# First queries on the ACT queue, half of each Q copy on GpSimd, and the ReLU tiles moved by 128 bytes

## The chip, the cores and the metric

The kernel runs on one core of one Trainium2 chip. The metric is the device time of one execution in microseconds (us); lower is better. The core has five engines that matter here: PE (TensorE, the matrix unit), DVE (VectorE), ACT (ScalarE), POOL (GpSimd) and SP (SyncE, which in this kernel only issues DMAs). Each runs its own instructions in order and waits on semaphores of the others.

## The reference

Two blocks follow each other, all in float32. The first is a gated linear recurrence over 4 batches, 8 heads, 768 positions and a head size of 48:

```python
for t in range(S):
    state = alpha[:, :, t, :, None] * state + np.einsum('bhd,bhe->bhde', k[:, :, t], v[:, :, t])
    y[:, :, t] = np.einsum('bhd,bhde->bhe', q[:, :, t], state)
```

Its output, with the heads laid side by side, is `x`, 3072 rows of 384. The second block is a mixture of four experts, whose shares are normalised probabilities:

```python
p = domain_probs / (domain_probs.sum(-1, keepdims=True) + 1e-09)
for e in range(E):
    h = np.maximum(x @ w1[e], 0.0)
    out += p[:, e:e + 1] * (h @ w2[e])
```

Here `w1[e]` is 384 by 1024 and `w2[e]` is 1024 by 384.

## The kernel before, in words

**Units and groups.** The recurrence is cut into 24 units, one for each chunk of 128 positions and each batch. Units are gathered into groups for the expert block: the first group has two units (256 rows of `x`), the next five have four (512 rows) and the last has two. A group can go through the experts when its units are done, and while the PE works on the experts of one group, the units of the next are worked off between its matmuls.

**One unit (`attention`, L273).** The generator loads alpha, K, Q and V of its chunk, and turns alpha, K and Q on the PE (L270) so that channels lie on partitions: `AT` (L281), `KT` (L286) and `QT` (L300, alpha times Q). Then it goes through seven levels, which double the distance over which the decays are multiplied up. At each level `copy_q` (L314) copies the half of `QT` that is needed into a block `qb`, in two copies of 64 partitions each (L321): heads are kept in pairs, and each member of a pair has its own half of the partitions and of the block. `next_q` (L324) multiplies the same half of `QT` in place (L328), so it has to wait until both copies have read the old values, and builds the next decays (L330). `next_k` (L333) copies one half of `KT` into a new tile (L340) and multiplies the other half into it (L341). The scores of a level come from the PE (`products`, L348) and are taken into `near` under a mask (`take`, L358, which reads `masks`); the last level writes `far` (L403) and the pieces are joined in `lat` (L416, L421). `result` multiplies them with V (L443) and ACT copies the outcome into the group's `x` (L459). `turn_keys` and L478 make the state for the next chunk.

For the first unit `alone` is true (L296): nothing else runs yet. Its KT copies at L340 already go to POOL (L339); its Q copies all go to ACT.

**Experts.** `up` computes `x @ w1` in tiles `one` and `two`, and `down` computes `h @ w2` (L650). From the second group on the numbers are split into parts that the PE's faster float32r form holds exactly enough: `one` and `two` at L557, then ACT copies `one` to `t` (L568), DVE adds `two` (L570), ACT writes the ReLU of `t` to `hT` (L595), and DVE makes two more parts of it in `hT` (L597, L603). `hT` is the tile of the ReLU values: four buffers from the pool `hid`. In `down` a block of 128 rows of `hT` is the stationary operand of the PE and 384 columns of `w2` are the moving one. The first group runs in plain float32 (L549, L551, and L650 on `hT` with no split).

**Weights.** In the first group, SP loads the pieces of `w1` straight from the input (L214, L215), four pieces of three DMAs of 128 KB; raw `w2` pieces land in unused parts of `hT` (L217). ACT and DVE split them, POOL writes the split form to a kept buffer in DRAM (L233), and later groups load it from there (L196).

**The start, in order.** ACT issues the DMAs of `ident` and `masks`. POOL clears tiles. SP issues alpha, K, Q (L167) and V (L172 to L174) of unit 0, then the same of unit 1, then the probabilities (L749), then the twelve DMAs of the first four `w1` pieces. Unit 1's alpha, K and Q land in one `hT` buffer. PE fills the time with matmuls on zeros (`idle`, L760), which are counted out by hand: 7 ahead of the turn of alpha, 2 ahead of that of K, 3 ahead of that of Q, 21 ahead of unit 1's first turn. Each of these is two records in the trace. After the first unit, `up` of the first group starts on the first 128 rows (L549).

**Memory.** Tiles lie in a partition in the order of the pools: `const`, `wts`, `work`, `hid`. The last tile of `work` is `x_raw`, and `hid` begins right behind it with the four buffers of `hT`, followed by `acc`.

Order is set by the program text (a manual schedule): on each engine, instructions stand as the generators are called.

Of the kernel before, what the change touches and what calls it, by code (L numbers as in the profile page):

```python
# [10 lines left out]
F32 = mybir.dt.float32  # L11
# [9 lines left out]
def kernel(  # L21
# [37 lines left out]
    nc = tc.nc  # L59

    B, H, S, D = q.shape
    E, DM, F = moe_w1.shape
    P = 128
# [5 lines left out]
    KC = DM // P  # L69
    FCH = F // P  # L70
    NT = B * P
# [6 lines left out]
    assert DM % P == 0 and F % (P * NQ) == 0 and DM <= 512 and KC * QF == FPQ * DM  # L78
    FINE = 1 + 1 / 4096
    TRIM = 1 - 1 / 8192  # L80

    j = np.arange(P)[:, None] % HALF
    n = np.arange(QUAD)[None, :]
    mask_np = np.stack([(j // (2 * m) == n // m) & (j % (2 * m) < m) for m in LEVELS[:6]],
                       1).astype(np.uint8)
# [5 lines left out]
    work = ctx.enter_context(tc.tile_pool(name="work", bufs=2))  # L91
# [5 lines left out]
    masks = const.tile([P, 6, QUAD], U8, name="masks")  # L97
# [33 lines left out]
    def raw(u, nm):  # L131
        return values[u % 2] if nm == "v" else apart[nm] if u == 1 else early[nm]

    xTs = {}
    xraws = {}
# [24 lines left out]
    def load(u, names):  # L160
        if u >= len(units):
            return
        cb, b = units[u]
        for nm in names:
            src = srcs[nm][b, :, cb * P:(cb + 1) * P, :].rearrange("h s d -> s h d")
            if nm != "v":
                nc.sync.dma_start(out=raw(u, nm)[:, :, :D], in_=src)  # L167
                continue

            pairs = raw(u, nm).rearrange("p (a i) d -> p a i d", i=2)  # L170
            src = src.rearrange("p (a i) d -> p a i d", i=2)
            nc.sync.dma_start(out=pairs[:, :, 0, :D], in_=src[:, :, 0])  # L172
            nc.sync.dma_start(out=pairs[:, :, 1, :TAIL], in_=src[:, :, 1, QUAD:])
            nc.sync.dma_start(out=pairs[:, :, 1, TAIL:D], in_=src[:, :, 1, :QUAD])  # L174
# [46 lines left out]
    def split_piece(l, i):  # L221
# [3 lines left out]

        nc.scalar.activation(out=top, in_=whole, func=ACT.Copy, scale=TRIM)
        yield
        nc.scalar.activation(out=dif, in_=whole, func=ACT.Copy, scale=TRIM * 4096)
        yield
# [43 lines left out]
    def attention(u):  # L273
        cb, b = units[u]
# [21 lines left out]
        alone = u == 0  # L296
# [17 lines left out]
        def copy_q(li):  # L314
            m = LEVELS[li]
            qv = halves(QT, m)[:, :, :, 1, :]
            qb = free.popleft()
            qbs.append(qb)
            for i in range(2):
                rows = slice(HD * i, HD * (i + 1))  # L320
                nc.scalar.copy(out=qb[rows, :, i, :].rearrange("p a (b r) -> p a b r", r=m),  # L321
                               in_=qv[rows])

        def next_q(li):  # L324
            m = LEVELS[li]
# [88 lines left out]
        for s in range(2):  # L414
            rows = slice(HALF * s, HALF * (s + 1))
            nc.scalar.copy(out=parts[:HALF, :, s, :, HALF:], in_=far[rows])  # L416
        yield
        for s in range(2):
            rows = slice(HALF * s, HALF * (s + 1))
            copy = nc.vector.tensor_copy if alone and s else nc.scalar.copy  # L420
# [8 lines left out]
        def result():  # L429
            yps = ps.tile([P, KC, P], F32, name="yps", tag="w")  # L430
            for c in range(KC):


                if c < 2:
                    now = [[(2 * c + j // 2, j % 2, (0, HD + TAIL)[j % 2], 2 * QUAD * (j % 2))
                            for j in range(4)]]
                    turns = ([(True, now[0])] if cb > 0 else []) + [(False, now[0])]
                else:
                    turns = [(True, [(p, 0, 0, QUAD) for p in range(NP)])] if cb > 0 else []
                    turns += [(False, [(p, i, QUAD + TAIL * i, 0) for p in range(NP)]) for i in range(2)]  # L440
                for n, (past, turn) in enumerate(turns):
                    for j, (p, i, in_v, in_st) in enumerate(turn):
                        nc.tensor.matmul(  # L443
                            yps[QUAD * j:QUAD * (j + 1), c, :],
                            lhsT=flat_st[:, p, in_st:in_st + QUAD] if past
                            else flat_v[:, p, in_v:in_v + QUAD],
                            rhs=QT[:, p, :] if past else lat[:, 2 * p + i, :],
                            start=(n == 0), stop=(n == len(turns) - 1))
            gi, slot = place[cb, b]
            if slot == 0:  # L450
                if gi == 0:
                    xTs[gi] = work.tile([P, 3, KC, NT], F32R, name="xT", bufs=1)
                    xraws[gi] = xTs[gi][:, 2].bitcast(F32)
                elif gi < LAST:
                    xraws[gi] = work.tile([P, KC, NT], F32, name="x_raw", bufs=1)
                else:
                    xraws[gi] = []
            if gi < LAST:
                nc.scalar.copy(out=xraws[gi][:, :, slot * P:(slot + 1) * P], in_=yps)  # L459
            else:  # L460

                xraws[gi].append(AT)
                nc.scalar.copy(out=AT[:, :KC, :], in_=yps)
# [10 lines left out]
        if cb < NCB - 1:  # L474
# [5 lines left out]
            for i in range(2):  # L480
                rows = slice(HD * i, HD * (i + 1))
# [17 lines left out]
    def split_x(gi, step):  # L499
# [7 lines left out]
        for kc in range(KC) if step == 0 else [step - 1]:  # L507
# [3 lines left out]
            for x, out in pieces:  # L511
                if step == 0:
                    nc.scalar.activation(out=out[0], in_=x, func=ACT.Copy, scale=TRIM)
                else:
# [78 lines left out]
    def hidden_parts(x, parts):  # L593
        top, low, dif = parts
        nc.scalar.activation(out=top, in_=x, func=ACT.Relu, scale=TRIM)  # L595
        yield
# [136 lines left out]

    with tc.manual_schedule():
        nc.scalar.dma_start(out=ident_all, in_=nc.inline_tensor(ident_np, name="ident_c").ap())
        nc.scalar.dma_start(out=masks, in_=nc.inline_tensor(mask_np, name="masks_c").ap())
        nc.gpsimd.memset(sts[B - 1], 0.0)
        for nm in "akq":
            for r in (early[nm], apart[nm]):
                nc.gpsimd.memset(r[:, :, D:], 0.0)  # L740
        nc.gpsimd.memset(lat[HALF:, :, :HALF], 0.0)
        for t in values + blocks:
            nc.gpsimd.memset(t, 0.0)
        for t in sts[:-1]:
            nc.gpsimd.memset(t, 0.0)

        load(0, "akqv")
        load(1, "akqv")
        nc.sync.dma_start(out=p_all, in_=moe_domain_probs.rearrange("(n p) e -> p n e", p=P))  # L749
        for i in range(NQ):  # L750
            load_piece(0, i)

        idle = ps.tile([P, P], F32, name="idle", tag="g", bufs=4)
        zeros = sts[B - 1].rearrange("p a i d -> p (a i d)")[:, :P]

        def fill(n):
            for _ in range(n):
                nc.tensor.matmul(idle, lhsT=zeros, rhs=zeros, start=True, stop=True)  # L760

        runs = [attention(u) for u in range(len(groups[0]))]
        fill(7)
        for u, n in ((0, 2), (0, 3), (0, 4), (0, 5), (0, 5), (0, 4), (0, 3), (1, 0), (0, 0), (0, 2),
                     (0, 2), (1, 2), (0, 2), (1, 0), (0, 0), (0, 4), (0, 4), (0, 0)):
            next(runs[u])
            fill(n)
        norm_probs()

        span = cost(0, 0, 0) * FCH / 2 + cost(1, 0, 0)  # L770
        waiting.extend((span * (k + 1) / 15, u, runs[u])
                       for k, u in enumerate([1, 1, 1, 0, 1, 0, *[1] * 8]))
        for fc in range(FCH):
            up(0, 0, fc, slice(0, 1))
            advance(cost(0, 0, 0) / 2)
        down(0, 0, [0], deque())
        while waiting:
            next(waiting.popleft()[2], None)
        clock = 0.0
        waiting.extend((1.0 + k, 1, runs[1]) for k in range(2))  # L780
        waiting.extend(deal())

        for (gi, e), after in zip(tasks, [*tasks[1:], (None, None)]):
            rest = gi == e == 0
            for fc in range(FCH):
                up(gi, e, fc, slice(1, len(groups[0])) if rest else None)
                advance(cost(0, gi, e) / (2 if rest else 1))
            each = len(groups[gi]) if split2(gi, e) else 1
            turns = [range(k, k + each) for k in range(rest, len(groups[gi]), each)]
            for k, slots in enumerate(turns):  # L790

                between = deque()
                if after[1] == 0:

                    for step, at in enumerate((0.0, 0.3, 0.42, 0.54) if gi == 0 else
                                              (0.0, 0.6, 0.7, 0.78)):
                        at = at * len(turns) - k
                        if 0 <= at < 1:
                            between.append((at, lambda step=step: split_x(after[0], step)))
                down(gi, e, slots, between)  # L800
        while stores:
            stores.popleft()()
# [28 lines left out]
```

## Time and profile before

| What | Value |
|---|---|
| Median of 4 runs | 1057.53 us |
| The runs | 1057.48, 1057.49, 1057.57, 1059.46 us |
| The profiled execution | 1059.58 us, of which the instructions span 1057.8 us |
| PE busy | 1039.5 us, 98% of the span |
| DVE, ACT, POOL busy | 782.0, 565.1, 35.5 us |
| Granted TensorE clock | 1.00 |
| DMA | 251.66 MB, mean 238 GB/s |
| `down` in float32r (L650) | 1872 matmuls, 347.4 us |
| `up` in float32r (L557) | 960 + 480 matmuls of the four-unit groups, 253.1 + 136.4 us |

In the profile a group of instructions is named by its line, its engine, its operation and out<-in tiles. `PEld` is the load of the stationary operand, which goes beside matmuls; `SPq` and `ACTq` are issues of DMAs by those engines. The mean duration of a matmul in the profile contains its way through the array, so the time that a row of matmuls takes is read from their starts, not from the mean. A releaser after `<-` names what ended an engine's idle time.

### The profile page before, as it was taken

To read this page: it belongs to the slowest core of one execution; us is meant where nothing else is said; L and a number is where in the kernel's file an instruction comes from. 1 tells how busy PE (TensorE), PEld (TensorE's weight loads), DVE (VectorE), ACT (ScalarE), POOL (GpSimd) and SP (SyncE) were. 2 spreads that over 40 slices of the span, in tenths; PEclk is the share of its full clock that TensorE was granted. 3 is DMA by queue.
4 is the path that set the end of the run, shared out by engine and by line. 5 is a ranking of instruction groups with operands and counts; after the bars stand their busy time and mean duration, and the time that the engine had idled before them with its cause. 6 is when DMAs were issued, how large, how long until landed. Compare 5 with 4: busy or idle time off the path is not lost.

```text
span 1057.8 us, 21578 instructions
## 1 busy us (share of the span) xinstructions
PE 1039.5 (98%) x8498; PEld 904.9 (86%) x8498; DVE 782.0 (74%) x1620; ACT 565.1 (53%) x1195; POOL 35.5 (3%) x77
## 2 busy tenths in 40 slices
PE   8899999999999999999999999999999999999998
PEld 8777777687877899898898898998989989898988
DVE  5578777668879778778877777986877875656565
ACT  4687776585665654445546536555474453323232
POOL 3000010000001000000000000000000000000000
PEclk9999999999999999999999999999999999999999
DMA  7596799997878956857759659576594454454531
GB/s 116 168 335 209 237 309 361 318 338 240 274 269 292 372 198 223 318 163 287 289 178 335 236 161 358 182 275 251 168 364 188 173 209 179 179 186 173 206 152 46
DMA packets 158837, 251.66 MB, mean 238 GB/s; under 512 B 120112, under 2 KB 135344, under 8 KB 136208
## 3 DMA queue, kind: packets, MB, share of 16 engines
q1 hardware_dynamic: 152688, 208.87, 57.9%
q0 software_dynamic: 5760, 41.29, 9.8%
q8 instruction: 67, 1.10, 0.4%
q14 instruction: 34, 0.28, 0.1%
q10 hardware_dynamic: 288, 0.12, 0.1%
HBM read 207.79 MB, written 42.47 MB: 237 GB/s over the span
## 4 chain that ended last, share of the span: by engine, by line
PE 82%; DMA 5%; DVE 4%; ACT 4%; SPq 3%; issue 1%; POOL 0%; ACTq 0%; DVEq 0%; POOLq 0%
PE ops L650 34%; PE one L557 23%; PE two L557 11%; PE sc L348 5%; PE yps L443 3%; PE tp L270 3%; SPq L214 2%; ACT qb L321 2%; DMA w<-in_moe_w_dram 2%; PE sps L478 1%; PE far L403 1%; PE one L549 1%; DMA w<-kept 1%; DMA kept<-w 1%; DMA rq<-in_q_dram 1%
## 5 line engine op out<-in xcount | busy, mean ns | idle before, releaser
L650 PE MATMUL ops<-w,hT 128*128 128x384 f32 x1872 | 347.4, 340 | 0.2 <-DVE hT L603 0.2
L650 PEld LDWEIGHTS ops<-w,hT 128*128 128x128 f32 x1872 | 325.4, 188 | 4.7 <-ACT t L568 0.6
L557 PE MATMUL one<-xT,w 128*128 128x512 f32 x960 | 253.1, 399 | 1.2 <-DVE xT L252 0.5
L557 PEld LDWEIGHTS one<-xT,w 128*128 128x128 f32 x960 | 175.8, 188 | 40.0 <-ACT t L568 1.5
L568 ACT ACTIVATE t<-one 128x512 f32<-128x512 f32 (+1 forms) x192 | 106.9, 557 | 176.2 <-PE one L557 170.8
L321 ACT COPY qb<-QT 64x256 f32<-64x256 f32 x336 | 136.5, 406 | 74.2 <-DVE QT L300 40.8
L597 DVE SCALAR_TENSOR_TENSOR hT<-t,hT 128x512 fp32r<-128x512 f32 (+1 forms) x172 | 110.5, 643 | 68.3 <-ACT hT L595 66.4
L570 DVE TENSOR_TENSOR t<-t,two 128x512 f32<-128x512 f32 (+1 forms) x172 | 109.4, 636 | 58.0 <-ACT t L568 29.1
L595 ACT ACTIVATE hT<-t 128x512 fp32r<-128x512 f32 (+1 forms) x172 | 101.8, 592 | 85.9 <-DVE t L570 84.9
L557 PE MATMUL two<-xT,w 128*128 128x512 f32 x480 | 136.4, 393 | 0.0
L557 PEld LDWEIGHTS two<-xT,w 128*128 128x128 f32 x480 | 90.1, 188 | 20.2 <-DVE acc L679 0.3
L603 DVE SCALAR_TENSOR_TENSOR hT<-hT 128x512 fp32r<-128x512 f32 (+1 forms) x172 | 101.0, 635 | 0.0
L650 PE MATMUL ops<-hT 128*128 128x384 f32 x288 | 100.6, 491 | 0.1
L358 DVE COPY_PREDICATED near<-masks,sc 128x256 f32<-128x256 uint8 x144 | 77.0, 535 | 19.2 <-PE sc L348 16.3
L328 DVE TENSOR_TENSOR QT<-QT,dec 128x256 f32<-128x256 f32 x144 | 61.1, 425 | 35.5 <-ACT qb L321 34.7
L348 PEld LDWEIGHTS sc<-qb,KT 128*64 128x64 f32 x2304 | 72.7, 138 | 9.3 <-issue 4.7
L348 PE MATMUL sc<-qb,KT 128*64 128x64 f32 x2304 | 77.2, 223 | 2.6 <-ACT qb L321 2.6
L650 PEld LDWEIGHTS ops<-hT 128*128 128x128 f32 x288 | 52.1, 190 | 29.1 <-issue 0.4
L679 DVE SCALAR_TENSOR_TENSOR acc<-ops,p_all,acc 128x384 f32<-128x384 f32 x82 | 49.9, 615 | 29.7 <-PE ops L650 28.5
L341 DVE TENSOR_TENSOR KT<-KT,dec 128x256 f32<-128x256 f32 x144 | 60.2, 418 | 0.0
L340 ACT COPY KT<-KT 128x256 f32<-128x256 f32 x138 | 57.4, 416 | 3.1
L549 PE MATMUL one<-xT,w 128*128 128x256 f32 (+1 forms) x240 | 46.8, 341 | 1.7 <-DMA w<-in_moe_w_dram 1.1
(90 smaller groups left out, 935.2 us busy)
## 6 DMA issues: line engine op xcount, KB each, us to landing
w<-kept SPq DMA_DIRECT2D x144, 1152.0 KB
kept<-w POOLq DMA_DIRECT2D x32, 1152.0 KB, 7.4
hT<-in_moe_w_dram SPq DMA_DIRECT2D x32, 384.0 KB
w<-in_moe_w_dram SPq DMA_DIRECT2D x48, 128.0 KB
ra<-in_alpha_dram SPq DMA_DIRECT2D x23, 192.0 KB
rk<-in_k_dram SPq DMA_DIRECT2D x23, 192.0 KB
rq<-in_q_dram SPq DMA_DIRECT2D x23, 192.0 KB
out_dram<-acc POOLq DMA_DIRECT2D x18, 192.0 KB, 6.7
```

The lines of the kernel that those rows point to most:

```text
L321: nc.scalar.copy(out=qb[rows, :, i, :].rearrange("p a (b r) -> p a b r", r=m), in_=qv[rows])
L328: nc.vector.tensor_mul(qv, qv, spread(dv[:, :, :, 0], m))
L341: nc.vector.tensor_mul(new[:, :, :, 0, :], old[:, :, :, 0, :], spread(halved(decs[li])[:, :, :, 1], m))
L348: nc.tensor.matmul(out[HALF * s:HALF * (s + 1), 2 * p:2 * p + 2, :], lhsT=KTs[li][:, p, HALF * s:HALF * (s + 1)], rhs=qbs[li][:, p, :, QUA ...
L358: nc.vector.copy_predicated(near.rearrange("p a (b two r) -> p a b two r", two=2, r=m)[:, :, :, 1, :], mk.unsqueeze(1).broadcast_to([P, H, ...
L557: nc.tensor.matmul(out, lhsT=w[:, part, kc], rhs=x_part(gi, part, kc), start=(part == terms[0] and kc == 0), stop=(part == terms[-1] and k ...
L568: nc.scalar.activation(out=t, in_=one, func=ACT.Copy, scale=FINE)
L570: nc.vector.tensor_add(t, t, two)
L595: nc.scalar.activation(out=top, in_=x, func=ACT.Relu, scale=TRIM)
L597: nc.vector.scalar_tensor_tensor(out=low, in0=x, scalar=0.0, in1=top.bitcast(F32), op0=ALU.max, op1=ALU.subtract)
L603: nc.vector.scalar_tensor_tensor(out=dif, in0=top.bitcast(F32), scalar=1 / 4096.0, in1=low.bitcast(F32), op0=ALU.mult, op1=ALU.subtract)
L650: nc.tensor.matmul(sums[at], lhsT=h, rhs=w, start=(n == begins[at]), stop=(n == ends[at]))
```

## The change

Three things are changed.

1. The DMA of unit 0's Q is issued by ACT instead of SP, behind that of `ident`. The DMA of `masks` moves from ACT to SP, behind the loads of unit 0 and ahead of those of unit 1.
2. In unit 0, the second of the two copies of each level's Q goes to POOL instead of ACT. There are seven levels, so seven copies of 64 partitions by 256 elements move.
3. `x_raw` gets 32 unused floats at its end. Everything behind it in a partition, the four buffers of `hT` and the accumulators `acc`, begins 128 bytes later. No other tile moves, and no instruction changes its shape for it.

The order of the instructions on PE, DVE and SP's other DMAs stays. On POOL the copies alternate: the Q copy of a level, then its KT copy.

```diff
+    PAD = 32
...
             if nm != "v":
-                nc.sync.dma_start(out=raw(u, nm)[:, :, :D], in_=src)
+
+                queue = nc.scalar if u == 0 and nm == "q" else nc.sync
+                queue.dma_start(out=raw(u, nm)[:, :, :D], in_=src)
                 continue
...
             for i in range(2):
                 rows = slice(HD * i, HD * (i + 1))
-                nc.scalar.copy(out=qb[rows, :, i, :].rearrange("p a (b r) -> p a b r", r=m),
-                               in_=qv[rows])
+                copy = nc.gpsimd.tensor_copy if alone and i else nc.scalar.copy
+                copy(out=qb[rows, :, i, :].rearrange("p a (b r) -> p a b r", r=m), in_=qv[rows])
...
                 elif gi < LAST:
-                    xraws[gi] = work.tile([P, KC, NT], F32, name="x_raw", bufs=1)
+                    xraws[gi] = work.tile([P, KC * NT + PAD], F32, name="x_raw", bufs=1)[:, :KC * NT]
+                    xraws[gi] = xraws[gi].rearrange("p (c n) -> p c n", n=NT)
...
         nc.scalar.dma_start(out=ident_all, in_=nc.inline_tensor(ident_np, name="ident_c").ap())
-        nc.scalar.dma_start(out=masks, in_=nc.inline_tensor(mask_np, name="masks_c").ap())
         nc.gpsimd.memset(sts[B - 1], 0.0)
...
         load(0, "akqv")
+        nc.sync.dma_start(out=masks, in_=nc.inline_tensor(mask_np, name="masks_c").ap())
         load(1, "akqv")
```

## The prediction

> **What bounds the kernel now.** I read the page's busy shares first, then the engines by stage, then PE's waits by stage.
>
> ```profile
> PE 1039.5 (98%) x8498; PEld 904.9 (86%) x8498; DVE 782.0 (74%) x1620; ACT 565.1 (53%) x1195; POOL 35.5 (3%) x77
> ```
>
> ```profile
> 0.00:24.30 24.30, 21.21 (x258) 20.08 (x258) 14.70 (x40) 11.20 (x23) 8.70 (x27) 1.00 0.81 115
> 24.30:60.00 35.70, 32.37 (x344) 26.13 (x346) 20.94 (x49) 25.15 (x63) 1.74 (x3) 1.00 0.68 200
> 60.00:165.00 105.00, 98.02 (x967) 75.30 (x964) 84.02 (x184) 78.48 (x173) 6.91 (x13) 1.00 0.84 277
> 165.00:1058.00 893.00, 887.91 (x6939) 783.35 (x6937) 662.31 (x1349) 450.31 (x937) 18.17 (x34) 1.00 0.66 238
> ```
>
> Columns are stretch, length, then busy time of PE, PEld, DVE, ACT, POOL. From 165 us on PE never rests: its waits there come to 1.1 us (0.5 + 0.4 + 0.2 in the waits of that stretch). So a faster or slower DVE, ACT or POOL changes nothing there; only the spacing of PE's own matmuls does. Ahead of 24.3 us PE mostly runs fillers, and unit 0 is a chain over DVE, ACT and POOL. Between lies one wait that matters for everything ahead of it; PE's timeline shows it, and the chain of work names the DMA behind it:
>
> ```profile
> 24.34 3.67 PE L549 MATMUL one<-xT,w 128*128 128x128 f32 x30 [0.59 <-ACT xT L459]
> 28.29 1.11 PE L549 MATMUL one<-xT,w 128*128 128x128 f32 x8
> 30.44 1.01 PE L549 MATMUL one<-xT,w 128*128 128x128 f32 x4 [1.05 <-DMA w<-in_moe_w_dram]
> ```
>
> ```profile
> 21.98 8.42 DMA w<-in_moe_w_dram
> ```
>
> PE could have gone on at 29.39 and waits 1.05 us for the fourth w1 piece. Whatever starts PE earlier only lengthens this wait; whatever starts it later costs nothing for the first 1.05 us.
>
> **The first Q on its own queue.** By the trace's completion events alpha lands at 4.36 us, K at 5.73, Q at 6.90. PE's timeline says whether Q was awaited:
>
> ```profile
> 4.49 1.09 PE L270 MATMUL tp<-ident,ra 128*128 128x128 f32 x4
> 6.07 0.60 PE L270 MATMUL tp<-ident,rk 128*128 128x128 f32 x4
> 6.50 0.83 PE L760 MATMUL idle<-st 128*128 128x128 f32 x6
> 7.17 0.60 PE L270 MATMUL tp<-ident,rq 128*128 128x128 f32 x4
> ```
>
> The six fillers run without a hole up to 7.17, where the turn of Q begins, 0.27 us after Q landed. An earlier Q therefore gains nothing. But alpha is used 0.13 us after landing and K 0.34 us, and Q now shares the 16 DMA engines with them. One such load is 1024 packets, and the packets move at 863 per us from 4 to 6 us. If Q's packets (from about 3.0 us, when ident's are out) take turns with alpha's rest and K's, alpha ends 0.25 to 0.45 us later and K 0.8 to 1.3 us later, the first at the 1130 packets per us that the slot from 3 to 4 us shows with two queues busy, the second at 863. After K's 0.34 us of room, the turn of K, the fillers and the turn of Q move by up to 1.0 us. Lower bound 0 (if Q's packets come after K's). I take +0.5.
>
> **The wall.** After unit 1's loads and the probabilities, the packets of w1 begin at 14.0 us; from 14 to 25 us only some 28% of the DMA engines' time is used by them, as if four or five engines carried them all, and the last needed one lands at 30.40. So the wall is the end of the small packets plus 16.4 us. Q's leaving SP's queue takes 1024 packets from it and masks add 128. If the second queue runs free, w1 starts (1024 - 128)/863 = 1.04 us earlier; if all share one throughput, masks' place at most costs 0.15 us. SP itself loses Q's issue (1.12 us) and gains one like masks' (0.45). I take -0.3, nearer to sharing, because the slot with two queues was only 31% faster and the overlap is about 1.8 us: 0.31 x 1.8 = 0.55 at best, half of it taken.
>
> The Trainium skill, "DMA: Bandwidth & Descriptors", section "Issuing engines are not separate DMA queues", says that DMAs of all issuers run on the same 16 engines and a second issuer saves only the sequencer's time. By that the wall would move by 0 instead of -0.3. The slot at 3 us (1130 against 863 packets) is slightly at odds with it.
>
> **The Q copies on POOL.** Before, a level of unit 0 is: QT multiplied (L328), two copies on ACT one behind the other, next QT.
>
> ```profile
> 10.09 0.86 ACT L321 COPY qb<-QT 64x256 f32<-64x256 f32 x2 [0.55 <-DVE QT L328]
> ```
>
> ```profile
> 10.98 0.52 DVE L328 TENSOR_TENSOR QT<-QT,dec 128x256 f32<-128x256 f32 x1 [0.31 <-ACT qb L321]
> 12.44 0.42 DVE L328 TENSOR_TENSOR QT<-QT,dec 128x256 f32<-128x256 f32 x1 [0.41 <-ACT qb L321]
> 13.86 0.62 DVE L328 TENSOR_TENSOR QT<-QT,dec 128x256 f32<-128x256 f32 x1
> ```
>
> ```profile
> 12.17 0.40 POOL L340 COPY KT<-KT 128x256 f32<-128x256 f32 x1 [0.94 <-DVE KT L341]
> 13.47 0.73 POOL L340 COPY KT<-KT 128x256 f32<-128x256 f32 x1 [0.90 <-DVE KT L341]
> ```
>
> DVE waits for the copies at two levels, 0.31 + 0.41 = 0.72 us. From 13.26 to 22.4 us it has no hole, so the other levels have nothing to give. With halves side by side a level's copy is 0.43 on ACT beside 0.40 to 0.73 on POOL instead of 0.86, so 0.13 to 0.46 saved a level, at most all of the 0.72. Against it stands POOL beside DVE: the KT copy grows from 0.40 to 0.73 and the same L328 from 0.42 to 0.52 and 0.62 where they overlap. Seven more POOL copies (levels 0 to 6), each costing DVE 0.1 to 0.2, are 0.7 to 1.4 us, and none where they fall into DVE's waits. Net between -0.72 and +1.4; I take 0. ACT's load of its table, behind Q's issue now, ends by about 4.4 us (Q's issue 1.12 and the 1.28 of the table), ahead of its first copy at 5.62. On POOL the KT copy now stands behind the Q copy of its level; what waits for it is L341 of the next level (POOL fills one half of the tile that L341 then reads), some 1.1 us later on DVE, so 0.4 to 0.7 us more before it are covered.
>
> The Trainium skill, "SBUF — State Buffer", section "SBUF: two separate sides", states that DVE with two SBUF inputs and a reading GpSimd instruction lock each other out for the whole instruction. By that rule seven copies of 0.42 would stop DVE for up to 2.9 us. The rows show 0.1 to 0.2 for an overlap, so I keep those.
>
> **Sum of the start.** Unit 0 moves by +0.5 + 0 = +0.5 us (from -0.72 to 1.0 + 1.4 = +2.4). Of that 1.05 is hidden by the wall; the wall moves by -0.3 (-1.04 to +0.15). Behind 30.4 us everything hangs on it: the larger of the two counts, max(-0.3, 0.5 - 1.05) = -0.3. Worst, 2.4 - 1.05 = +1.35; best, -1.04.
>
> **The 128 bytes.** `hT` is PE's stationary operand at L650 and is written by ACT (L595) and DVE (L597, L603). Writers have slack behind 165 us, so only PE's spacing counts. Two unbroken rows of 96 matmuls in the timeline, of one shape:
>
> ```profile
> 916.92 16.81 PE L650 MATMUL ops<-w,hT 128*128 128x384 f32 x96
> 933.56 0.87 PE L557 MATMUL one<-KT,w 128*128 128x256 f32 x6
> ...
> 967.97 17.12 PE L650 MATMUL ops<-w,hT 128*128 128x384 f32 x96
> 984.92 0.87 PE L557 MATMUL one<-KT,w 128*128 128x256 f32 x6
> ```
>
> From start to next start, (933.56 - 916.92)/96 = 173.3 ns and (984.92 - 967.97)/96 = 176.6 ns. Over all undisturbed neighbours the mean is 175.3, and grouped by buffer and place of `hT` it stays between 174.4 and 176.4 with a single outlier, with both spacings in most groups. So the two spacings are not a matter of the address within what the trace has; but all `hT` blocks there lie 512 bytes apart, so the trace has nothing on a step of 128. Bounds: all 1872 at 173.3, 1872 x -2.0 ns = -3.7 us; all at 176.6, 1872 x +1.3 = +2.4 us. I take 0, since the addresses that do differ make no difference.
>
> **Sum.** The profiled execution took 1059.58 us (span 1057.8), 2.05 above the median of 1057.53; another run lies up there too, at 1059.46. The parts work on differences, so I set them against the median: 1057.53 - 0.3 + 0 = 1057.2.
>
> **Rivals.**
> - *The start is swallowed and the shift does nothing* (forecast): 1057.2. For it: PE's 1.05 us wait, no trace of addresses. Chance 0.46, with the start's own range 1056.5 to 1058.9. About 0.2% (2.1 us) is what a measurement of this kernel can tell from no change, so this is "same".
> - *The shift puts `down` into the short spacing.* Then 1057.2 - 3.7 = 1053.5. It counts as faster from about half of that on. For it: the short spacing exists for the same shape; against it, the mixture in every place of `hT`. Chance 0.33.
> - *The shift puts `down` into the long spacing, so it gets slower.* Place: L650; 1057.2 + 2.4 = 1059.6, beyond 0.2% only if nearly all 1872 matmuls take it; a step in L650 of more than 1.3 ns does it as well. Chance 0.17.
> - *The copies on POOL and the late K together outrun the wall.* Here K's DMA decides: with the turn of K 1.0 us late and DVE 1.4 us slower, +1.35: 1058.9. Within the measurement unless DVE is stopped for whole copies. Chance 0.04, counted as slower.
>
> **Numbers.** Faster 0.33, same 0.46, slower 0.21. The range takes the best of both parts, 1057.53 - 1.04 - 3.7 = 1052.8, and the worst, 1057.53 + 1.35 + 2.4 = 1061.3.
>
> **What the new profile would show.** The turn of Q at 7.5 to 8.2 us instead of 7.17, or earlier if alpha and K are not held up. POOL with 13 copies in unit 0; L328 without its 0.31 and 0.41 waits, but longer than 0.42. The wait at the fourth w1 piece still there, ending near 30.1. L650's rows of 96 at 173.3 or 176.6. I am wrong if the wait at that piece is gone, if L650's spacing leaves these two values, or if PE's waits between 30 and 165 us change by more than a microsecond.

## The result and the profile after

The changed kernel takes 1056.75 us (median of 42 runs) against 1058.2 us for the kernel before (60 runs, taken beside it): a ratio of 0.9988, 95% interval 0.9983 to 0.9993. That is 1.3 us less, inside the 0.2% that was called "same", and 1.0 us beyond the step of -0.3 us that was forecast. The near hit is not a merit of its parts: two of them were far off, in opposite directions.

The traced execution took 1056.44 us, near its median; that of the kernel before (1059.58 us) lay 1.4 us above its own. So a second trace of the kernel before was taken later (1057.52 us), and where a few tenths count, both are given. The page of the changed kernel, and its engines by stage:

```profile
PE 1035.9 (98%) x8498; PEld 901.0 (85%) x8498; DVE 782.4 (74%) x1620; ACT 561.8 (53%) x1188; POOL 39.8 (4%) x84
```

```profile
0.00:24.30 24.30, 20.23 (x246) 19.23 (x250) 15.01 (x38) 7.66 (x15) 12.95 (x34) 1.00 0.79 115
24.30:60.00 35.70, 32.44 (x351) 25.89 (x342) 21.01 (x50) 24.85 (x62) 1.74 (x3) 1.00 0.67 194
60.00:165.00 105.00, 98.55 (x979) 75.44 (x976) 84.33 (x186) 79.31 (x175) 7.45 (x14) 1.00 0.84 280
165.00:1054.70 889.70, 884.68 (x6940) 780.48 (x6938) 662.00 (x1349) 450.03 (x937) 17.65 (x33) 1.00 0.66 239
```

ACT's seven copies are POOL's now (84 instructions against 77). The last stage got 3.3 us shorter against the first trace of before, with nearly the same waits on PE (1.3 us for 1.1); the start got later. PE's timeline of the start:

```profile
4.45 0.73 PE L274 MATMUL tp<-ident,ra 128*128 128x128 f32 x4
6.86 0.63 PE L274 MATMUL tp<-ident,rk 128*128 128x128 f32 x4 [1.23 <-DMA rk<-in_k_dram]
7.99 0.60 PE L274 MATMUL tp<-ident,rq 128*128 128x128 f32 x4
25.45 3.62 PE L554 MATMUL one<-xT,w 128*128 128x128 f32 x30 [0.59 <-ACT xT L464]
29.34 1.06 PE L554 MATMUL one<-xT,w 128*128 128x128 f32 x8
30.61 1.06 PE L554 MATMUL one<-xT,w 128*128 128x128 f32 x4 [0.22 <-DMA w<-in_moe_w_dram]
32.01 1.13 PE L483 MATMUL sps<-rv,AT 128*128 128x96 f32 x8 [0.34 <-ACT AT L472]
```

K is awaited for 1.23 us, and unit 0's chain reaches the first L554 (L549 before) 1.11 us later than in the first trace of before, 1.36 later than in the second. The wait for the fourth w1 piece has shrunk from 1.05 to 0.22 us, as it should if it hides a late start. But right behind it stands a wait that neither trace of before has: `sps` for ACT's copy of the turned keys. And `down`, four rows of 96 matmuls at the end, always in the short spacing (two of them shown):

```profile
864.67 16.81 PE L655 MATMUL ops<-w,hT 128*128 128x384 f32 x96
881.32 0.89 PE L562 MATMUL one<-KT,w 128*128 128x256 f32 x6
...
965.89 16.80 PE L655 MATMUL ops<-w,hT 128*128 128x384 f32 x96
982.53 0.89 PE L562 MATMUL one<-KT,w 128*128 128x256 f32 x6
```

(881.32 - 864.67)/96 = 173.4 ns and (982.53 - 965.89)/96 = 173.3 ns. Over all neighbours that run back to back the mean is 173.3 ns against 175.0 before. (Such means are worked out from the starts of the matmuls in the traces, leaving out neighbours whose distance in time is more than 30 ns off 175 ns, or off 230 ns for 512 columns.)

### The profile page after: what moved, and what is told of

It reads as the page before. It is cut to its first block, busy times and chain, and to the rows that moved or that the text cites. A ratio compares the mean times of both kernels' runs of the same rounds, so it can differ in the third digit from the quotient of the medians.

```text
span 1054.7 us, 21584 instructions
## 1 busy us (share of the span) xinstructions
PE 1035.9 (98%) x8498; PEld 901.0 (85%) x8498; DVE 782.4 (74%) x1620; ACT 561.8 (53%) x1188; POOL 39.8 (4%) x84
## 4 chain that ended last, share of the span: by engine, by line
PE 84%; DVE 6%; ACT 4%; DMA 2%; issue 2%; SPq 1%; POOL 0%; DVEq 0%; ACTq 0%; POOLq 0%
PE ops L655 35%; PE one L562 23%; PE two L562 11%; PE sc L352 5%; PE yps L447 3%; PE tp L274 3%; ACT qb L326 2%; PE one L554 2%; PE sps L483 1%; PE far L407 1%; DMA w<-kept 1%; DVE w L234 1%; DMA rq<-in_q_dram 1%; DVE QT L332 1%; ACT KT L344 1%
## 5 line engine op out<-in xcount | busy, mean ns | idle before, releaser
L573 ACT ACTIVATE t<-one 128x512 f32<-128x512 f32 (+1 forms) x192 | 107.0, 557 | 173.3 <-PE one L562 168.3
L326 ACT COPY qb<-QT 64x256 f32<-64x256 f32 x329 | 133.7, 406 | 77.1 <-DVE QT L304 40.9
L554 PE MATMUL one<-xT,w 128*128 128x256 f32 (+1 forms) x240 | 46.7, 341 | 0.9 <-ACT xT L464 0.6
```

Source lines behind the costliest of these rows:

```text
L573: nc.scalar.activation(out=t, in_=one, func=ACT.Copy, scale=FINE)
```

## The experiments

Each is the kernel before with the edit that is shown or named. Three theories stood at the beginning: A, that the place of the ReLU tiles sets the spacing of `down` and the start costs; B, that any change of the start deals the spacings anew; C, that the start gives the gain.

### The 128 bytes alone

```diff
-                    xraws[gi] = work.tile([P, KC, NT], F32, name="x_raw", bufs=1)
+                    xraws[gi] = work.tile([P, KC * NT + 32], F32, name="x_raw", bufs=1)[:, :KC * NT]
+                    xraws[gi] = xraws[gi].rearrange("p (c n) -> p c n", n=NT)
```

> The 32 unused floats behind x_raw alone, everything else as before. Theory A (the place of the ReLU tiles sets the spacing of the down matmuls): their mean spacing falls from 175.0 ns to 173.3 +- 0.3 ns as with the whole change, and the time is 1.2 to 2.2 us below before, somewhat more than the whole change gave, since the start's loss is not paid. Theory B (the mixture of 173.3 and 176.6 ns is a matter of phase that any change of the start deals anew): the mixture stays near that of before, since the start is untouched, and the time is within 0.5 us of before. Theory C (the start gives the gain): time as before.

Measured: 1055.26 us against 1058.13, ratio 0.9976 (0.9967 to 0.9985), that is -2.5 us; spacing 173.3 ns. This is the lowest median of the study, and a larger gain than that of the whole change. Theory A holds, B and C fall.

### The start alone

Parts 1 and 2 of the change, without the floats behind `x_raw`.

> Q's DMA on ACT's queue, masks on SP's, half of unit 0's Q copies on POOL, but x_raw without the 32 floats. Theory A: down spacing 174.5 to 175.5 ns as before, time 0 to 0.8 us above before; the waits of the start as in the changed kernel (K awaited for 1.2 us, far at about 20.0 us). Theory B: spacing 173.3 ns, time about 1.2 us below before. Theory C: time about 1.2 us below before with spacing as before.

Measured: 1059.54 us, ratio 1.002 (1.001 to 1.003): +2.1 us, more than expected. Spacing 174.7 ns, 36% of the neighbours in the long form, a mixture like that of the kernel before (45% and 41% in its two traces; long form: 176 ns and more). The start's half of the change is a loss. Its PE timeline shows the place, once more the keys:

```profile
6.83 0.63 PE L271 MATMUL tp<-ident,rk 128*128 128x128 f32 x4 [0.47 <-DMA rk<-in_k_dram]
...
25.44 3.62 PE L550 MATMUL one<-xT,w 128*128 128x128 f32 x30 [0.59 <-ACT xT L460]
28.89 0.60 PE L271 MATMUL tp<-ident,KT 128*128 128x128 f32 x4
29.32 1.52 PE L550 MATMUL one<-xT,w 128*128 128x128 f32 x12
32.00 1.13 PE L479 MATMUL sps<-rv,AT 128*128 128x96 f32 x8 [1.16 <-ACT AT L468]
```

At the fourth w1 piece PE does not wait here at all: twelve matmuls run on from 29.32. What it did not wait there it waits 1.16 us at `sps`, for ACT.

### The queue alone

```diff
-                nc.sync.dma_start(out=raw(u, nm)[:, :, :D], in_=src)
+                queue = nc.scalar if u == 0 and nm == "q" else nc.sync
+                queue.dma_start(out=raw(u, nm)[:, :, :D], in_=src)
...
-        nc.scalar.dma_start(out=masks, in_=nc.inline_tensor(mask_np, name="masks_c").ap())
...
         load(0, "akqv")
+        nc.sync.dma_start(out=masks, in_=nc.inline_tensor(mask_np, name="masks_c").ap())
```

> Only the DMAs of Q and masks change places. If K's late landing makes the start late (theory A): the turn of K begins at 6.8 to 6.9 us instead of 6.07, everything in unit 0 shifts by 0.8 us, the first L549 begins at about 25.1 us instead of 24.34 and the fourth w1 piece is awaited for about 0.3 us instead of 1.05. Time +0.2 to +0.6 us against before. Rival: the second queue brings w1 earlier, the wait for the fourth piece ends before 30.2 us and the time is below before.

Measured: 1059.21 us, ratio 1.0008 (0.9998 to 1.0018): +0.8 us, not told from zero for certain. Its PE timeline:

```profile
6.92 0.63 PE L271 MATMUL tp<-ident,rk 128*128 128x128 f32 x4 [1.30 <-DMA rk<-in_k_dram]
25.22 3.62 PE L550 MATMUL one<-xT,w 128*128 128x128 f32 x30 [0.59 <-ACT xT L460]
30.61 0.49 PE L550 MATMUL one<-xT,w 128*128 128x128 f32 x2 [0.22 <-DMA w<-in_moe_w_dram]
31.76 1.13 PE L479 MATMUL sps<-rv,AT 128*128 128x96 f32 x8 [0.67 <-ACT AT L468]
```

By the completion events K lands at 6.79 us and Q at 6.29, where before they landed at 5.73 and 6.90: Q gained 0.6 us that nobody waits for, and K lost 1.1 that PE does wait for. The fourth w1 piece comes no earlier (30.61 against 30.44 and 30.04), so the rival of an earlier w1 falls.

The packets of the trace fit that. From 3 to 5 us 2014 packets start here, 1002 of them on the second queue, against 1993 with 144 on the second queue before: the two queues share one rate. The piece's time also varies from execution to execution: with the start alone, above, on the same two queues, it was there by 30.2.

### The copies alone, twice

```diff
-                nc.scalar.copy(out=qb[rows, :, i, :].rearrange("p a (b r) -> p a b r", r=m),
-                               in_=qv[rows])
+                copy = nc.gpsimd.tensor_copy if alone and i else nc.scalar.copy
+                copy(out=qb[rows, :, i, :].rearrange("p a (b r) -> p a b r", r=m), in_=qv[rows])
```

> Only the seven Q copies go to POOL. Theory A: DVE's waits of 0.31 and 0.41 us at QT go, POOL beside DVE gives about as much back; the turn of K stays at 6.07 us, the first L549 begins between 24.0 and 24.8 us, and the wall at 30.44 us stands, so the time is within 0.3 us of before. Rival (the copies shorten the start for good): first L549 at 23.6 us or earlier. Rival (POOL stops DVE for whole copies): first L549 later than 25.5 us.

> The Q copies on POOL alone, a second execution with more rounds. The first had the time 0.4 to 2.1 us above before, while its trace shows PE 0.1 us ahead of before at 36 us. If the copies cost time, it is again 0.5 to 2 us above before and the trace shows where PE loses; if it was chance, within 0.4 us of before.

Measured: 1058.96 us, ratio 1.0012 (1.0004 to 1.0021) the first time, 1058.15 us, ratio 0.9999 (0.999 to 1.0008) the second. The loss of the first did not come again, and neither trace shows one behind 36 us; no gain is there either. Inside unit 0, DVE's timeline tells why:

```profile
9.41 0.53 DVE L328 TENSOR_TENSOR QT<-QT,AT 128x256 f32<-128x256 f32 x1
10.20 0.64 DVE L341 TENSOR_TENSOR KT<-KT,AT 128x256 f32<-128x256 f32 x1
11.09 0.51 DVE L330 TENSOR_TENSOR dec<-dec 128x128 f32<-128x128 f32 x1
12.22 0.42 DVE L328 TENSOR_TENSOR QT<-QT,dec 128x256 f32<-128x256 f32 x1 [0.29 <-POOL qb L322]
13.24 0.89 DVE L374 TENSOR_TENSOR near<-ident,dot 128x512 f32<-128x512 f32 x1
```

Before, these took 0.43, 0.42, 0.28, 0.42 (behind a wait of 0.41) and 0.68 us. From the first L300 to the sum of the probabilities (L257) DVE goes from 7.75 to 22.61, 14.86 us, against 14.56 (7.89 to 22.45) before and 14.55 in the second trace: 0.3 us longer, where its waits got 0.5 us shorter and its work 0.8 us longer (busy 14.32 against 13.49 in such a stretch). POOL's copies beside them, and an instruction of DVE that reads one tile only:

```profile
8.59 0.59 POOL L322 COPY qb<-QT 64x256 f32<-64x256 f32 x1 [2.01 <-DVE QT L300]
9.24 0.41 POOL L340 COPY KT<-KT 128x256 f32<-128x256 f32 x1
10.07 0.48 POOL L322 COPY qb<-QT 64x256 f32<-64x256 f32 x1 [0.41 <-DVE QT L328]
10.97 0.48 POOL L340 COPY KT<-KT 128x256 f32<-128x256 f32 x1 [0.42 <-DVE KT L341]
13.65 0.74 POOL L340 COPY KT<-KT 128x256 f32<-128x256 f32 x1
```

```profile
8.94 0.55 DVE L292 TENSOR_REDUCE dot<-t 128x8 f32<-128x384 f32 x1
```

The Trainium skill, "SBUF — State Buffer", section "SBUF: two separate sides", has the two engines lock each other out for whole instructions, where DVE's has two inputs in SBUF and GpSimd's reads there: the one that starts first keeps the other waiting. The rows agree. An instruction that begins while a copy runs waits for what is left of the copy, not for a whole one. At 9.41 the copy had 0.24 us left, and L328 grew by 0.10; at 10.20 and 11.09 it had 0.35 and 0.36 left, and L341 and L330 grew by 0.22 and 0.23: each time the rest less 0.13 or 0.14 us. The other way round, the copy of 13.65 began with 0.48 us of L374 left and took 0.74 instead of 0.40. L292, with one input, began with 0.24 us of a copy left and took 0.55 as before.

### By 256 and by 512 bytes

The same edit as with 128 bytes, with 64 and with 128 floats.

> 64 unused floats behind x_raw instead of 32, nothing else changed: the ReLU tiles begin 256 bytes later. Theory A1 (what counts is the start within 256 bytes): the spacing of the down matmuls stays at 174.7 to 175.1 ns with 35 to 45% in the long form, time as before. Theory A2 (what counts is the distance to the w2 tiles or the start within a longer period): spacing may fall to 173.3 ns, time 2 to 3 us below before.

> 128 unused floats behind x_raw: the ReLU tiles begin 512 bytes later, one whole block of 128 float columns. Theories A1 and A2 with a period of up to 512 bytes: spacing 174.7 to 175.1 ns as before, time as before. If the spacing is 173.3 ns, any shift from the old place does it, and the period is longer than 512 bytes.

Measured: by 256 bytes 1058.06 us, ratio 0.9998 (0.9988 to 1.0008). Of its ten executions only one was traced, and that one took 5419 us, with 615 ns from matmul to matmul in `down`, so its spacing is not known: that 256 bytes change nothing is shown by the time alone. By 512 bytes 1058.54 us, ratio 1.0003 (0.9994 to 1.0013), spacing 174.8 ns. Not any shift does it; neither of these two whole numbers of 256 bytes changes the time.

### All tiles moved, and all but the ReLU tiles

```diff
     ident = ident_all[:, :P]
+    gap = const.tile([P, 32], F32, name="gap")
```

moves every working tile by 128 bytes. With 96 floats more behind `x_raw` (the edit above), the ReLU tiles are moved by 512 in all, so they stay where they were within 256 bytes while `w1`, `w2` and `x` have moved by 128.

> An unused tile of 128 bytes behind ident in the first pool and nothing behind x_raw: every working tile, w1 and w2 and x with the ReLU tiles, begins 128 bytes later. Theory A1 (the ReLU tiles' own place): spacing 173.3 ns, time about 2.5 us below before. Theory A2 (their distance to the w2 tiles): spacing 174.7 to 175.1 ns, time as before.

> The 128 unused bytes behind ident and 96 unused floats behind x_raw: w1, w2, x and the work tiles begin 128 bytes later, the ReLU tiles 512 bytes later. Theory A1: the ReLU tiles are at the same place within 256 or 512 bytes as before, so spacing 174.7 to 175.1 ns. Theory A2: their distance to w2 has changed by 384 bytes, that is by 128 the other way within 512, so the spacing may change; if it falls to 173.3 ns here and not when all moves, the distance counts.

Measured: all moved, 1058.27 us, ratio 1.0003 (0.999 to 1.0015), spacing 174.8 ns. All but the ReLU tiles, 1055.53 us, ratio 0.9979 (0.9968 to 0.999), spacing 173.3 ns; in its traced execution, one wait for the kept weights at 166 us lasted 2.8 us, so the page of that one is of no use for the total. This settles it: with the ReLU tiles at the good place and `w2` moved along, nothing is won; with the ReLU tiles at the old place and `w2` moved, all of it. What counts is the distance of the stationary operand from the moving one. The place of the ReLU tiles by itself (A1) falls.

### Half the shift

The edit of 128 bytes with 16 floats instead of 32.

> 16 unused floats behind x_raw: the distance between the ReLU tiles and the w2 tiles, taken within 256 bytes, is 128 instead of 64 (before) or 192 (with the change). If the distance works as a switch at half of the 256 bytes, the spacing goes to 173.3 ns and the time to about 2.5 us below before; if only 192 is good, the mixture stays at 174.7 to 175.1 ns and the time as before; a mean between the two would mean a gradual effect.

Measured: 1059.99 us, ratio 1.0018 (1.0007 to 1.003); spacing 175.9 ns, worse than the mixture of before: 68% of the neighbours at 174 to 176 ns and 16% at 181 and more, where the kernel before has under 1%. A row of its timeline, (882.82 - 865.93)/96 = 175.9 ns:

```profile
865.93 17.06 PE L651 MATMUL ops<-w,hT 128*128 128x384 f32 x96
882.82 0.87 PE L558 MATMUL one<-KT,w 128*128 128x256 f32 x6
```

The rise of 1.1 ns over the 174.8 of the second trace of before is 2.0 us over 1872 matmuls; the time rose by 1.9.

### The same distance for `up`

```diff
                 if gi == 0:
+                    gap = work.tile([P, 32], F32, name="gap", bufs=1)
                     xTs[gi] = work.tile([P, 3, KC, NT], F32R, name="xT", bufs=1)
```

> The 128 unused bytes lie ahead of x instead of behind x_raw: x and the ReLU tiles begin 128 bytes later, w1 and w2 stay. The distance of the ReLU tiles to w2 is that of the change, so down should space at 173.3 ns. New is the distance of x (moving) to w1 (stationary) in the up matmuls, 192 instead of 64 within 256 bytes: if the distance of the two operands matters in general, the mean spacing of the up matmuls of 512 columns leaves 229.4 to 229.9 ns, and could go down to 226 or up to 233 ns, which is -5 to +5 us over 1440 matmuls; if it matters for down alone, it stays and the time is about 2.5 us below before.

Measured: 1059.89 us, ratio 1.0019 (1.001 to 1.0028). `down` spaces at 173.4 ns, but the `up` matmuls of 512 columns go from 229.7 (second trace of before) to 233.2 ns. That is 1872 x -1.5 = -2.7 us and 1440 x +3.6 = +5.1 us, together +2.4; the time rose by 2.0. In rows of the timeline, nine matmuls of `up`: first the kernel before (second trace), (951.69 - 949.63)/9 = 229 ns, then this one, (954.39 - 952.29)/9 = 233 ns.

```profile
949.63 1.54 PE L557 MATMUL one<-xT,w 128*128 128x512 f32 x6
951.00 0.85 PE L557 MATMUL two<-xT,w 128*128 128x512 f32 x3
951.69 1.54 PE L557 MATMUL one<-xT,w 128*128 128x512 f32 x6
```

```profile
952.29 1.56 PE L558 MATMUL one<-xT,w 128*128 128x512 f32 x6
953.69 0.86 PE L558 MATMUL two<-xT,w 128*128 128x512 f32 x3
954.39 1.56 PE L558 MATMUL one<-xT,w 128*128 128x512 f32 x6
```

### The kernel before, a second trace

> The kernel before, unchanged, for a second trace of it. If the long and the short spacing are dealt by the addresses alone, the share of long spacings in down is 45% again; if chance has a part in it, it is nearer to the 36 to 41% of the kernels that leave the addresses alone. The wait for the kept weights at 164 us may differ from 0.3 us by up to some tenths.

Measured: 1057.52 us; 41% of `down`'s neighbours in the long form, mean 174.8 ns. So at the old distance the two spacings are mixed, and the mixture differs from execution to execution (30 to 45% over the traces that have this distance). PE did not wait at the kept weights at 164 us; in other traces it waited 0.1 to 2.8 us there, by chance of the DMAs, which is a part of why single runs differ by a microsecond or two.

### The distance, in one table

The tiles' places in a partition follow from the pools: `hT` begins at byte 172000 before, `w2` at 49056, `x` at 147424, `w1` at 85920; the buffers of each lie whole multiples of 256 bytes apart. The columns and rows that single matmuls take begin at whole multiples of 256 bytes in their tiles, so all 1872 of `down` have one distance. Distance is the stationary operand's start less the moving one's, within 256 bytes.

| Kernel | `down`: hT less w2 | mean spacing | `up`: w1 less x | mean spacing |
|---|---|---|---|---|
| before (two traces) | 64 | 175.0, 174.8 ns | 192 | 229.9, 229.7 ns |
| by 512 bytes | 64 | 174.8 | 192 | 229.6 |
| all by 128 | 64 | 174.8 | 192 | 229.8 |
| half the shift | 128 | 175.9 | 192 | 229.4 |
| 128 bytes alone | 192 | 173.3 | 192 | 229.4 |
| all but hT by 128 | 192 | 173.3 | 192 | 229.3 |
| x and hT by 128 | 192 | 173.4 | 64 | 233.2 |

At 192 `down` takes 173.3 to 173.4 ns and `up` 229.3 to 229.9; at 64, 174.8 to 175.0 and 233.2. That `up` goes by the distance too rests on one kernel. Distances of 0 and those that are no multiple of 64 were not tried.

## Why the prediction was right and where it was not

**What bounds the kernel** held: behind 165 us only the spacing of PE's own matmuls changed, and PE's waits there stayed 1.1 us apart from one of 0.2 for kept weights.

**The first Q on its own queue: right in kind and size.** Q's earlier landing gained nothing and K came later. K landed at 6.72 us, 1.0 later (0.8 to 1.3 was said); its turn moved by 0.8 (up to 1.0, +0.5 taken). Alpha was not held up: 4.31 against 4.36. The turn of Q began at 7.99 us, within the 7.5 to 8.2 that was said.

**The wall: wrong in the step "the last needed one lands" earlier by 0.3.** It landed no earlier, 30.61 against 30.44 and 30.04. The sum by the skill's rule ("DMA: Bandwidth & Descriptors", section "Issuing engines are not separate DMA queues"), a move of 0, was the better one. The 1130 packets of the slot at 3 us were misread as the rate of two queues: only 144 of them were on the second one. In the changed kernel 622 of that slot's are, and there are 1130 again; from 3 to 5 us it moves 1985 packets against 1993. The first packets of 1 KB, those of w1, start at 14.16 us, against 14.40 and 13.89 in the two traces of before (the prediction had 14.0).

**The copies: mechanism right, the term mis-sized by 0.3.** 0 was taken for the net; it is +0.3 us in unit 0: 0.5 saved in waits, 0.8 lost by instructions of DVE that overlap POOL. The 0.29 left at one level is the POOL copy, which ends later than ACT's. The 2.9 us that the prediction drew from the skill's rule took every copy to stop DVE for its whole length; an instruction that meets a copy waits for its rest, and that is what the rows of 0.1 to 0.2 had shown already.

**The sum of the start: wrong in the step "Behind 30.4 us everything hangs on it".** Of 1.05 us only 0.3 to 0.5 were to be had in the two traces of before. ACT goes on with unit 1 while PE waits at the wall, and that row of ACT hangs on unit 0. The copy that `sps` needs shows it, first before (second trace), then changed:

```profile
30.00 0.58 ACT L467 COPY AT<-tp 128x512 f32<-128x512 f32 x1
```

```profile
31.38 0.58 ACT L472 COPY AT<-tp 128x512 f32<-128x512 f32 x1
```

Before, it ended at 30.58 and PE needed it at 30.84: 0.26 us of room (0.47 in the first trace). So the start's 1.11 to 1.36 us came through as 0.7 to 1.2 us at `sps`, and PE's matmuls stay 0.8 us (first trace) to 1.3 us (second) behind up to 120 us.

Even that room is not there in most executions. In all traces but that of 5419 us ACT's copy ends 6.5 us after the first matmul of `up` begins. Of the six other kernels that leave the start alone and were traced, each begins `sps` 0.05 us behind the copy, because the fourth w1 piece did not come late enough to hide anything. The kernel with all tiles moved by 128 bytes, for one, never awaits the piece:

```profile
30.96 1.13 PE L479 MATMUL sps<-rv,AT 128*128 128x96 f32 x8 [1.15 <-ACT AT L468]
```

In the eight traces with the old start `up` begins at 24.42 us and `sps` at 31.04 in the mean (30.68 to 31.41); in the two with the new one `up` at 25.45 and 25.44, `sps` at 32.01 and 32.00. So about 1.0 us comes through, nearly all of the delay, and the fourth piece as a wall was a matter of the two traces of before. The timed loss of the start alone is 2.1 us, 1.1 to 3.2; what of it goes beyond these 1.0 to 1.3 us, the traces do not show.

**The 128 bytes: wrong in the step "I take 0, since the addresses that do differ make no difference".** It measured -2.5 us (-3.5 to -1.6), inside the bound of -3.7 and the rival with a chance of 0.33. The reason was unsound: the blocks compared lay multiples of 512 bytes apart, and the period is 256, so they could not have told. All 1872 at 173.3 ns is what came: 1872 x (175.0 - 173.3) = 3.2 us by the first trace, 2.8 by the second. The rival's price of 3.7 went from a mean of 175.3 ns, which the starts of the matmuls give as 175.0.

**The sum.** -2.5 for the shift and +2.1 for the start make -0.4; the whole change measured -1.3 (-1.8 to -0.7). The intervals of the two parts (each about 1 us to either side) allow that. Forecast was -0.3 for reasons that were both not so: a start that costs nothing and a shift that does nothing. The case that took place was the rival "The shift puts `down` into the short spacing", with half of its gain lost at the start; the rival that slows the start was underrated. The range of 1052.8 to 1061.3 held the time because it was built from both bounds.

## What to carry to other kernels

A wait that hides a delay hides it only for the engine that waits: before counting it as room, follow what the other engines do meanwhile, and find the next thing that PE needs from them. And a wait for a DMA that one trace shows may be missing in the next. A load on a second queue takes its share of the DMA engines from the first one's, so it should not be one that is needed last. And where PE is busy without a hole, the distance of the two operands of its float32r matmuls is worth a trial of a few bytes: here it is 1% of each matmul, and 128 bytes of padding alone gave -2.5 us where the whole change gave -1.3.

## What was not expected of the hardware

- The spacing of back-to-back float32r matmuls depends on the distance of the stationary operand from the moving one, within 256 bytes: 173.3 ns at 192, a mixture around 174.8 at 64, 175.9 at 128 for 384 columns; 229.3 to 229.9 and 233.2 ns at 192 and 64 for 512 columns. Moving both alike changes nothing. Why was not shown.
- At a distance of 64, the share of long spacings of one and the same program differs between executions (45% and 41%).
- A DVE instruction with two inputs that began inside a POOL copy grew by what was left of the copy less some 0.14 us (0.42 to 0.64 and 0.28 to 0.51 with 0.35 and 0.36 left, 0.43 to 0.53 with 0.24 left); one with a single input did not grow (0.55).
- Half of the packets on a second DMA queue made no more of them: 1985 from 3 to 5 us, 1003 of them on the second queue, against 1993 with 144.
